# First product of an item in a linear-attention and MoE kernel: the block products in pY and the last one in pZ stand at the item's end, behind the last one in pX

## The chip, the cores and the metric

The kernel runs on one core of one Trainium2 chip. The metric is the device time of one execution in microseconds (us); of the three runs of the kernel before, the median is 851.96 us (850.62 to 854.63). Engines are named as in the profile: PE is TensorE (PEld its weight loads), DVE is VectorE, ACT is ScalarE, POOL is GpSimd, SP is SyncE, which issues most of the transfers.

## The reference

Linear attention (q is normalised by a softmax over the head dimension, k by one over the sequence) is followed by a feed-forward pair of products with a gate between them. All inputs are float32; there are 8 batches of 576 tokens, so 4608 tokens of width 512, and 2048 hidden columns.

```python
kv = np.einsum('bhsd,bhse->bhde', softmax(k, axis=seq), v)
x = np.einsum('bhsd,bhde->bhse', softmax(q, axis=dim), kv)   # to (4608, 512)
h = x @ w_in                                                # 512 -> 2048
sp = np.maximum(h, 0.0) + np.log1p(np.exp(-np.abs(h)))
g = h * erf(sp)
out = g @ w_out                                             # 2048 -> 512
```

## The kernel before

**Items.** The work on h, g and out is cut into 48 items, numbered n = 0 to 47 in the order in which they run: 12 blocks of 384 tokens, and for each block 4 groups of 512 hidden columns. Items 0 to 3 compute in fp32 (`mm1_32`, line 1030). Items 4 to 47 go through `mm1(n, k)` (line 977), which is called four times for an item, with k = 0 to 3. Every fp32 product is put together from fp16 halves, three matmuls for one.

**First product.** For one item, h is 512 columns by 384 tokens. It is cut into 2 by 2 blocks, `C[i, j]`, where i is a half of the columns and j a half of the tokens, and computed by a scheme in the manner of Strassen: seven block products of pre-added operands in place of eight. One block product, `prod(b, wi, xi)`, is 12 matmuls of 128x192 into one of three PSUM banks, whose tiles are named pX, pY and pZ. Each bank has one buffer in its pool (`bufs=1`) and belongs to an item from its first product to the last read of it. Products into the same bank accumulate: an item's first product in a bank starts it, the later ones add to what is there. So bank pX takes four products of an item (operands 0-0, 3-6, 5-5, 2-4 in this order), and after each one its contents are copied or added into one block of the item's tile H in SBUF; bank pZ takes two (6-3 and 4-2) and bank pY one (1-1). The next product into a bank has to wait until the eviction of the one before has read the bank. The evictions of k = 0, 2 and 3 run on DVE (but for the last one of pX), those of k = 1 and the last one of pX on ACT.

**The gate.** `softplus` (line 1062) and `erf` (line 1071) run on ACT over the item's 128x1536 values, both through `act` (line 337; its instructions are at line 342 in the profile). They use different function tables, so a table load stands ahead of each. For the items of the middle block of each pair (n modulo 12 from 4 to 7) the softplus is done in two halves, by token half; each half reads the blocks of H of that token half only. Then DVE multiplies (`gmul`, line 1081), casts the high half (`ghi`, 1093) and subtracts it for the low half (`glo`, 1097). `gh` and `gl` lie in the tile H.

**Second product.** `mm2(n, tt)` (line 1103, matmuls at 1125) is, for each of three 128-token tiles, 12 matmuls of 128x512 into banks o0, o1, o2, which accumulate over the block's four items. After a block's last item DVE scales them into `ob` (line 1141) and SP stores them.

**Order.** The loop at lines 1225 to 1244 writes, for each n, the gmul of item n-1, then for i = 0 to 3: m n.i (the call `mm1(n, i)`), the casts of item n-1, the second product of item n-2, tile i, and some steps of the attention of a later pair of batches (`pace`); at the end the softplus and erf of item n. The order of the text is a priority: a scheduler decides what stands where on each engine. `wlast[0]` is the instruction behind which an attention step is placed (`behind(wlast[0])`). The attention steps use all engines: exps on ACT (line 342), normalisation and splitting of kv on DVE (lines 459 to 465, 565 to 600), transposing transfers on SP (line 647), products x and xt on PE (line 636), and the preparation of the operands of the block products (lines 287, 288, 386).

Of the kernel before, what the change touches and what calls it, by code (L numbers as in the profile page):

```python
# [14 lines left out]
ALU = mybir.AluOpType  # L15
# [42 lines left out]
def attn_moe_kernel(  # L58
# [9 lines left out]
    nc = tc.nc  # L68
# [166 lines left out]
    def wop(jn, h, i, n):  # L235

        o = h * WIN + i * 512
        return wplace[wjobs[jn]][:, o:o + n * 512].rearrange("p (n c f) -> p n c f", n=n, c=2)
# [51 lines left out]
    wlast = [None]  # L290
# [686 lines left out]
    def mm1(n, k):  # L977

        p, bk, g = seq[n]
        s = st[n]
        assert ("in", g) in wready
        x = x7[p * NBK + bk]
        jn = wjobs.index(("in", g))
        Th = T // 2
        if k == 0:
            s["H"] = ch.tile([P, FG, T], F32, tag="H", bufs=3, name=f"H_{n}")
        C = {(i, j): s["H"][:, 2 * i:2 * i + 2, Th * j:Th * j + Th]
             for i in range(2) for j in range(2)}  # L990

        def prod(b, wi, xi):
            new = b not in s
            if new:
                s[b] = psh.tile([P, 512], F32, tag=f"p{b}", name=f"p{b}_{n}")
            w = [wop(jn, h, wi, 1)[:, 0] for h in range(2)]
            for a in range(2):
                o = s[b][:, a * Th:(a + 1) * Th]
                for c in range(2):
                    for i, (wl, xl) in enumerate(((0, 0), (0, 1), (1, 0))):  # L1000
                        nc.tensor.matmul(  # L1001
                            o, w[wl][:, c, a * P:(a + 1) * P], x[:, xl, xi, c, :],
                            start=(new and a == 0 and c == 0 and i == 0),
                            stop=(c == 1 and i == 2), skip_group_check=True,
                        )

        def bank2(b):
            return s[b][:, :T].rearrange("p (a t) -> p a t", a=2)

        add = nc.vector.tensor_tensor  # L1010
        if k == 0:
            prod("Y", 1, 1)
            wlast[0] = nc.vector.tensor_copy(C[0, 0], bank2("Y")).ins  # L1013
            prod("X", 0, 0)
            add(C[0, 0], bank2("X"), C[0, 0], op=ALU.add)  # L1015
        elif k == 1:
            prod("Z", 6, 3)
            nc.scalar.copy(C[1, 1], bank2("Z"))  # L1018
            prod("X", 3, 6)
            nc.scalar.copy(C[0, 1], bank2("X"))  # L1020
        elif k == 2:
            prod("X", 5, 5)
            wlast[0] = add(C[1, 1], bank2("X"), C[1, 1], op=ALU.add).ins  # L1023
        else:
            prod("Z", 4, 2)
            wlast[0] = add(C[0, 1], bank2("Z"), C[0, 1], op=ALU.add).ins  # L1026
            prod("X", 2, 4)
            nc.scalar.copy(C[1, 0], bank2("X"))  # L1028

    def mm1_32(n, a):  # L1030

# [120 lines left out]
    def tok(name):  # L1152
# [20 lines left out]
        if c == "w":  # L1173
            warm(*x)
        elif c == "D":
            wdecode(NPC * x[0] + x[1], *x[2:])
        elif c == "Q":
            wsquares(*x)
        elif c == "S":
            wsplit(*x)  # L1180
        elif c == "R":
            wsplit_sums(*x)
        elif c == "f":
            xready(x_next[0])
            finish(x[0] % 2)
        elif c == "Z":
            wscales()
        elif c == "m":
            (mm1_32 if x[0] < NG else mm1)(*x)
            emitted.add(("m", *x))  # L1190
        elif c == "M":
            mm2(*x)
            emitted.add(("M", *x))
        else:
            fn[c](*x)
# [81 lines left out]
```

## Time and profile before

| | before |
|---|---|
| median of 3 runs | 851.96 us |
| the profiled execution | 851.51 us |
| its span in the profile | 849.5 us |
| ACT busy | 503.1 us (59%) |
| matmuls of the first product into pX, pZ, pY | 204.8, 103.8, 52.0 us |
| matmuls of the second product (line 1125) | 366.1 us |

Busy time is the time in which an engine worked on instructions; of two engines that are both busy for most of the span, only waits and order tell which one sets the pace. In the 40 slices of the span each digit is the busy share of one slice of about 21 us, in tenths. A row of a timeline has the start in us from the span's start, the duration in us of the row (of all instructions that it groups, xN), engine, line, operation, output and inputs with their shapes; the bracket behind it says how long the engine was idle just before and what released it. A row of the list of waits has the us waited in total, how many times, and the longest one. The chain of work that ended last is PE for 47% of the span, DVE for 24% and ACT for 13%.

### The profile page before, as it was taken

Reading aid. Unit: us, or ns where it says so; the run is one execution under the profiler, and the core shown is the slowest. Engines: PE = TensorE matmul, PEld = TensorE weight load, DVE = VectorE, ACT = ScalarE, POOL = GpSimd, SP = SyncE. Lnnn points to the kernel's source line nnn. Section 1 sums busy time; section 2 is a strip of 40 time slices with the busy share of each in tenths; the row PEclk is TensorE's granted clock in tenths of the full one; section 3 lists DMA queues with packets and bytes.
Section 4 is the critical chain, followed back from the end, with each engine's and each line's share of the span. In section 5 each row is a group of like instructions: output and inputs, shape, how many; then the busy total and the mean of one; then the engine's idle time right before and its main releaser. Section 6 shows DMA issues by size and latency. Waiting matters only on the chain.

```text
span 849.5 us, 15212 instructions
## 1 busy us (share of the span) xinstructions
PE 802.6 (94%) x6377; PEld 546.7 (64%) x6377; DVE 637.7 (75%) x883; ACT 503.1 (59%) x633; POOL 35.3 (4%) x51
## 2 busy tenths in 40 slices
PE   3999997989989999999999999999999999999997
PEld 2555557566667567666676766666776676777673
DVE  5999789998979697848966777848968557553543
ACT  2598587686565665564854567465763565543532
POOL 1012010000100000000000100000000000000000
PEclk8999999999999999999999999999999999999999
DMA  9996320015405601531153300431131000100101
GB/s 264 404 276 182 106 74 15 1 25 107 112 18 114 149 2 26 119 75 26 39 104 75 89 16 16 115 88 26 38 51 38 33 7 2 38 1 2 38 1 38
DMA packets 145508, 62.59 MB, mean 74 GB/s; under 512 B 134688, under 2 KB 136736, under 8 KB 145440
## 3 DMA queue, kind: packets, MB, share of 16 engines
q1 hardware_dynamic: 143264, 53.23, 25.6%
q0 software_dynamic: 2176, 8.39, 2.8%
q8 instruction: 50, 0.82, 0.4%
q14 instruction: 18, 0.15, 0.0%
HBM read 45.09 MB, written 9.44 MB: 64 GB/s over the span
## 4 chain that ended last, share of the span: by engine, by line
PE 47%; DVE 24%; ACT 13%; issue 11%; DMA 3%; SPq 2%; POOL 0%; ACTq 0%; DVEq 0%; POOLq 0%
PE o L1125 20%; PE pX L1001 12%; PE pZ L1001 6%; ACT G L342 5%; ACT L342 5%; DVE G L1081 3%; PE pY L1001 2%; DVE H L1097 2%; DVE H L1093 2%; PE x L636 2%; SPq L407 1%; DVE x L288 1%; PE o L1116 1%; DVE q L453 1%; DVE x L386 1%
## 5 line engine op out<-in xcount | busy, mean ns | idle before, releaser
L1125 PE MATMUL o<-wo,H 128*128 128x512 f16 x1584 | 366.1, 379 | 2.9 <-DVE H L1093 2.0
L1001 PEld LDWEIGHTS <-wi 128*128 128x128 f16 x3696 | 311.2, 98 | 54.7 <-issue 24.7
L1125 PEld LDWEIGHTS <-H 128*128 128x128 f16 x1584 | 152.1, 98 | 157.3 <-DVE H L1093 2.7
L1001 PE MATMUL pX<-x,wi 128*128 128x192 f16 x2112 | 204.8, 247 | 11.5 <-DVE H L1023 3.3
L342 ACT ACT_TABLE_LOAD x104 | 133.4, 1283 | 11.3 <-DVE H L1026 9.6
L1081 DVE SCALAR_TENSOR_TENSOR G<-G,small,H 128x1536 f32<-128x1536 f32 x44 | 79.9, 1816 | 66.9 <-ACT G L342 66.9
L1028 ACT COPY H<-pX 128x384 f32<-128x384 f32 x44 | 20.9, 475 | 152.0 <-PE pX L1001 152.0
L1001 PE MATMUL pZ<-x,wi 128*128 128x192 f16 x1056 | 103.8, 248 | 2.9 <-ACT H L1018 2.1
L342 ACT ACTIVATE G<-H,U 128x768 f32<-128x768 f32 (+1 forms) x60 | 72.9, 1231 | 22.1 <-DVE H L1026 21.5
L1097 DVE TENSOR_TENSOR H<-G,H 128x1536 f16<-128x1536 f32 x44 | 77.2, 1755 | 0.9
L342 ACT ACTIVATE G<-G 128x1536 f32<-128x1536 f32 x48 | 71.2, 1484 | 0.5
L1001 PE MATMUL pY<-x,wi 128*128 128x192 f16 x528 | 52.0, 247 | 3.1 <-DVE H L1013 3.1
L1026 DVE TENSOR_TENSOR H<-pZ,H 128x384 f32<-128x384 f32 x44 | 24.3, 552 | 35.2 <-PE pZ L1001 35.0
L1013 DVE COPY H<-pY 128x384 f32<-128x384 f32 x44 | 24.3, 552 | 29.8 <-PE pY L1001 29.8
L288 DVE SCALAR_TENSOR_TENSOR x<-x,x 128x768 f16<-128x768 f32 (+1 forms) x44 | 37.2, 852 | 11.9 <-ACT x L287 11.6
L441 ACT ACTIVATE x<-x 128x384 f32<-128x384 f32 (+1 forms) x52 | 17.5, 388 | 44.6 <-PE x L636 41.3
L1116 PE MATMUL o<-wo,G 128*128 128x512 f32 x96 | 43.6, 597 | 0.0
L1093 DVE CAST H<-G 128x1536 f16<-128x1536 f32 x44 | 42.0, 956 | 0.8
L287 ACT ACTIVATE x<-x 128x768 f16<-128x768 f32 (+1 forms) x44 | 32.8, 762 | 9.4 <-DVE x L386 9.3
L1141 DVE TENSOR_SCALAR ob<-o,V 128x512 f32<-128x512 f32 x29 | 21.7, 747 | 20.0 <-PE o L1125 19.9
L1015 DVE TENSOR_TENSOR H<-pX,H 128x384 f32<-128x384 f32 x44 | 24.3, 552 | 11.3 <-PE pX L1001 11.1
L1116 PEld LDWEIGHTS o<-wo,G 128*128 128x128 f32 x96 | 17.5, 190 | 18.5 <-issue 17.5
(175 smaller groups left out, 751.1 us busy)
## 6 DMA issues: line engine op xcount, KB each, us to landing
out_dram<-ob SPq DMA_DIRECT2D x32, 256.0 KB, 2.4
vbuf<-in_v_dram SPq DMA_DIRECT2D x60, 128.0 KB, 3.0
q<-in_q_dram SPq DMA_DIRECT2D x56, 128.0 KB, 3.4
k<-in_k_dram SPq DMA_DIRECT2D x56, 128.0 KB, 3.0
wo<-in_moe_w_in_dram SPq DMA_DIRECT2D x4, 1024.0 KB, 17.1
wi<-in_moe_w_out_dram POOLq DMA_DIRECT2D x2, 1024.0 KB, 7.0
wi<-in_moe_w_in_dram SPq DMA_DIRECT2D x2, 1024.0 KB, 8.5
raw<-in_moe_w_out_dram POOLq DMA_DIRECT2D x2, 1024.0 KB, 7.7
```

What stands on the lines that cost most here:

```text
L287: nc.scalar.activation(hi, src, AF.Copy, scale=s)
L288: return nc.vector.scalar_tensor_tensor(lo, src, s, hi, op0=ALU.mult, op1=ALU.subtract)
L342: i = nc.scalar.activation(out_, in_, func, **kw)
L1001: nc.tensor.matmul(o, w[wl][:, c, a * P:(a + 1) * P], x[:, xl, xi, c, :], start=(new and a == 0 and c == 0 and i == 0), stop=(c == 1 and i ...
L1013: wlast[0] = nc.vector.tensor_copy(C[0, 0], bank2("Y")).ins
L1015: add(C[0, 0], bank2("X"), C[0, 0], op=ALU.add)
L1026: wlast[0] = add(C[0, 1], bank2("Z"), C[0, 1], op=ALU.add).ins
L1081: nc.vector.scalar_tensor_tensor(flat(s["G"]), flat(s["G"]), GA[:, g:g + 1], flat(s["H"]), op0=ALU.mult, op1=ALU.mult,)
L1093: nc.vector.tensor_copy(flat(s["gh"]), flat(s["G"]))
L1097: nc.vector.tensor_tensor(flat(s["gl"]), flat(s["G"]), flat(s["gh"]), op=ALU.subtract)
L1116: nc.tensor.matmul(o, s["G"][:, a, ts_], w[:, a, :], start=(first_ and a == 0), stop=(last_ and a == FG - 1),)
L1125: nc.tensor.matmul(o, s[gt][:, a, ts_], w[wl][:, a, :], start=(first_ and a == 0 and i == 0), stop=(last_ and a == FG - 1 and i == 2),)
```

## The change

Only the order of the products and the kinds of three evictions in `mm1` change.

```diff
--- before.py
+++ after.py
@@ -1009,10 +1009,8 @@
 
         add = nc.vector.tensor_tensor
         if k == 0:
-            prod("Y", 1, 1)
-            wlast[0] = nc.vector.tensor_copy(C[0, 0], bank2("Y")).ins
             prod("X", 0, 0)
-            add(C[0, 0], bank2("X"), C[0, 0], op=ALU.add)
+            wlast[0] = nc.vector.tensor_copy(C[0, 0], bank2("X")).ins
         elif k == 1:
             prod("Z", 6, 3)
             nc.scalar.copy(C[1, 1], bank2("Z"))
@@ -1022,10 +1020,12 @@
             prod("X", 5, 5)
             wlast[0] = add(C[1, 1], bank2("X"), C[1, 1], op=ALU.add).ins
         else:
+            prod("X", 2, 4)
+            nc.scalar.copy(C[1, 0], bank2("X"))
+            prod("Y", 1, 1)
+            add(C[0, 0], bank2("Y"), C[0, 0], op=ALU.add)
             prod("Z", 4, 2)
             wlast[0] = add(C[0, 1], bank2("Z"), C[0, 1], op=ALU.add).ins
-            prod("X", 2, 4)
-            nc.scalar.copy(C[1, 0], bank2("X"))
 
     def mm1_32(n, a):
```

The product into pY (operands 1-1) leaves k = 0 and goes to k = 3, behind the last product of pX and ahead of the last one of pZ. With it the first write into C[0, 0] becomes the copy of bank pX, and bank pY is added. In k = 3 the last product into pX comes first and the last one into pZ last. `wlast[0]` is the copy of pX in k = 0 and the add of pZ in k = 3. The number of matmuls, copies and adds stays.

The lines of the changed kernel shift: the copy of pX is line 1013 there, pZ's and pX's copies of k = 1 are 1016 and 1018, the add of k = 2 is 1021, and the three of k = 3 are 1024 (pX, ACT), 1026 (pY, DVE) and 1028 (pZ, DVE). Lines below 1028 are the same.

How the change moves instructions is seen first on DVE at the end of the program, in items 46 and 47, where no attention work is left (H_46 and H_47 are the items' tiles, G_46 the gate's). Before:

```order
L1026 TENSOR_TENSOR H_46_7956<-pZ_46_7999,H_46_7956 128x2x192
L1013 COPY H_47_8096<-pY_47_8097 128x2x192
L1015 TENSOR_TENSOR H_47_8096<-pX_47_8111,H_47_8096 128x2x192
L1081 SCALAR_TENSOR_TENSOR G_46_8092<-G_46_8092,small_82,H_46_7956 128x1536
L1093 CAST H_46_7956<-G_46_8092 128x1536
L1097 TENSOR_TENSOR H_46_7956<-G_46_8092,H_46_7956 128x1536
L1023 TENSOR_TENSOR H_47_8096<-pX_47_8111,H_47_8096 128x2x192
```

and now:

```order
L1026 TENSOR_TENSOR H_46_7956<-pY_46_8065,H_46_7956 128x2x192
L1028 TENSOR_TENSOR H_46_7956<-pZ_46_7985,H_46_7956 128x2x192
L1013 COPY H_47_8096<-pX_47_8097 128x2x192
L1081 SCALAR_TENSOR_TENSOR G_46_8092<-G_46_8092,small_82,H_46_7956 128x1536
L1093 CAST H_46_7956<-G_46_8092 128x1536
L1097 TENSOR_TENSOR H_46_7956<-G_46_8092,H_46_7956 128x1536
L1021 TENSOR_TENSOR H_47_8096<-pX_47_8097,H_47_8096 128x2x192
```

The copy of item 47's pY stood between item 46's last add and the gate's multiplication of item 46; now pY's add belongs to item 46 itself and stands ahead of the add of pZ, and item 47 has one operation fewer ahead of that multiplication.

The second place is ACT from the last copy of item 25 on (x7_7 are operands of the block products of a later block, k_6 and q_6 the keys and queries of a later batch). Before:

```order
L1028 COPY H_25_4555<-pX_25_4570 128x2x192
L287 ACTIVATE x7_7_4768<-x_7_3461 128x768
L342 ACT_TABLE_LOAD
L342 ACTIVATE G_25_4734<-H_25_4555,U_4_3279 128x1536
L287 ACTIVATE x7_7_4768<-x_7_3461 128x768
L342 ACT_TABLE_LOAD
L342 ACTIVATE G_25_4734<-G_25_4734 128x1536
L1018 COPY H_26_4738<-pZ_26_4786 128x2x192
L1020 COPY H_26_4738<-pX_26_4753 128x2x192
```

and now:

```order
L1024 COPY H_25_4555<-pX_25_4556 128x2x192
L287 ACTIVATE x7_7_4754<-x_7_3447 128x768 x2
L342 ACT_TABLE_LOAD
L342 ACTIVATE G_25_4734<-H_25_4555,U_4_3265 128x1536
L342 ACT_TABLE_LOAD
L342 ACTIVATE G_25_4734<-G_25_4734 128x1536
L1016 COPY H_26_4738<-pZ_26_4772 128x2x192
L1018 COPY H_26_4738<-pX_26_4739 128x2x192
```

The second operation of line 287 moved from between softplus and erf to a place ahead of the softplus's table load. One item later, before:

```order
L1018 COPY H_27_4894<-pZ_27_4939 128x2x192
L342 ACT_TABLE_LOAD
L342 ACTIVATE k_6_0_4404<-k_6_0_4404 128x1024
L1020 COPY H_27_4894<-pX_27_4909 128x2x192
L342 ACTIVATE k_6_1_4409<-k_6_1_4409 128x1024
L342 ACTIVATE kt_3_4414<-kt_3_4414 64x512
```

and now:

```order
L1016 COPY H_27_4894<-pZ_27_4925 128x2x192
L1018 COPY H_27_4894<-pX_27_4895 128x2x192
L342 ACT_TABLE_LOAD
L342 ACTIVATE k_6_0_4390<-k_6_0_4390 128x1024
L342 ACTIVATE k_6_1_4395<-k_6_1_4395 128x1024
L342 ACTIVATE kt_3_4400<-kt_3_4400 64x512
```

The copy of pX stood between two exps of the keys and now stands ahead of the table load of the first.

The third place is DVE in item 29, where the attention's kv is split (kvbd0; U and V are scales). Before:

```order
L599 TENSOR_SCALAR kvbd0_86<-kvf_6_5145,x6_s_5372 64x4x64 x2
L1141 TENSOR_SCALAR ob_27_2_5367<-o_24_2_4848,V_4_5258 128x512
L600 SCALAR_TENSOR_TENSOR kvbd0_86<-kvf_6_5145,x6_s_5372,kvbd0_86 64x4x64 x2
L1026 TENSOR_TENSOR H_29_5215<-pZ_29_5265,H_29_5215 128x2x192
L970 TENSOR_SCALAR V_6_7269<-small_82,x6_u_5373 128x1
L1013 COPY H_30_5414<-pY_30_5415 128x2x192
L645 TENSOR_TENSOR k_6_1_4409<-q_6_1_4694,k_6_1_4409 128x1024
L1015 TENSOR_TENSOR H_30_5414<-pX_30_5429,H_30_5414 128x2x192
L1081 SCALAR_TENSOR_TENSOR G_29_5409<-G_29_5409,small_82,H_29_5215 128x1536
```

and now:

```order
L599 TENSOR_SCALAR kvbd0_86<-kvf_6_5131,x6_s_5358 64x4x64
L1141 TENSOR_SCALAR ob_27_2_5353<-o_24_2_4834,V_4_5244 128x512
L600 SCALAR_TENSOR_TENSOR kvbd0_86<-kvf_6_5131,x6_s_5358,kvbd0_86 64x4x64
L599 TENSOR_SCALAR kvbd0_86<-kvf_6_5131,x6_s_5358 64x4x64
L970 TENSOR_SCALAR V_6_7255<-small_82,x6_u_5359 128x1
L600 SCALAR_TENSOR_TENSOR kvbd0_86<-kvf_6_5131,x6_s_5358,kvbd0_86 64x4x64
L1026 TENSOR_TENSOR H_29_5215<-pY_29_5382,H_29_5215 128x2x192
L1028 TENSOR_TENSOR H_29_5215<-pZ_29_5251,H_29_5215 128x2x192
L1013 COPY H_30_5414<-pX_30_5415 128x2x192
L645 TENSOR_TENSOR k_6_1_4395<-q_6_1_4680,k_6_1_4395 128x1024
L1081 SCALAR_TENSOR_TENSOR G_29_5409<-G_29_5409,small_82,H_29_5215 128x1536
```

The add of pZ of item 29 stood behind the two operations of line 600; now the adds of pY and of pZ both do, and one of line 599 and that of line 970 moved between the two of line 600.

## The prediction

> **What bounds the kernel now.** I read first the page's busy shares and 40 slices, then PE's list of waits, then the timeline of a quiet item near the end, and the busy times by stretch.
>
> ```profile
> PE 802.6 (94%) x6377; PEld 546.7 (64%) x6377; DVE 637.7 (75%) x883; ACT 503.1 (59%) x633; POOL 35.3 (4%) x51
> PE   3999997989989999999999999999999999999997
> DVE  5999789998979697848966777848968557553543
> ```
>
> PE is busy 94% of 849.5 us and in nine tenths of nearly every slice: in most places only work taken from PE or a wait of PE changes the time. DVE, at 75% overall, is as full as PE in slices 6 to 12 (107 to 255 us), so there the two take turns at setting the pace. PE's waits name the possible gains:
>
> ```profile
> PE pX L1001 <- DVE H L1023: 3.3, 4, 1.4
> PE pX L1001 <- ACT H L1020: 3.1, 4, 1.2
> PE pX L1001 <- ACT H L1028: 2.8, 3, 1.3
> PE xt L636 <- DVE H L1023: 2.7, 2, 1.4
> PE xt L636 <- DMA qt<-kt: 2.1, 1, 2.1
> ```
>
> Below, product names follow the evictions: X0, X3, X5 and X4 are the four products in pX in order of execution (old lines 1015, 1020, 1023, 1028), Z1 and Z2 those in pZ (1018, 1026), Y that in pY (1013). A quiet item in old order:
>
> ```profile
> 811.81 1.15 PE L1001 MATMUL pX<-x,wi 128*128 128x192 f16 x12
> 813.00 0.48 ACT L1028 COPY H<-pX 128x384 f32<-128x384 f32 x1 [7.67 <-PE pX L1001]
> 813.50 1.28 ACT L342 ACT_TABLE_LOAD   x1
> 817.68 1.48 ACT L342 ACTIVATE G<-G 128x1536 f32<-128x1536 f32 x1
> 819.19 1.82 DVE L1081 SCALAR_TENSOR_TENSOR G<-G,small,H 128x1536 f32<-128x1536 f32 x1 [3.66 <-ACT G L342]
> 819.55 0.48 ACT L1020 COPY H<-pX 128x384 f32<-128x384 f32 x1
> 821.05 0.96 DVE L1093 CAST H<-G 128x1536 f16<-128x1536 f32 x1
> 821.94 1.15 PE L1001 MATMUL pX<-x,wi 128*128 128x192 f16 x12
> 822.04 1.76 DVE L1097 TENSOR_TENSOR H<-G,H 128x1536 f16<-128x1536 f32 x1
> 822.93 2.75 PE L1125 MATMUL o<-wo,H 128*128 128x512 f16 x12
> 823.72 0.55 DVE L1023 TENSOR_TENSOR H<-pX,H 128x384 f32<-128x384 f32 x1
> 825.52 1.15 PE L1001 MATMUL pZ<-x,wi 128*128 128x192 f16 x12
> 826.51 1.15 PE L1001 MATMUL pX<-x,wi 128*128 128x192 f16 x12
> ```
>
> X4 starts at 811.81 and again at 826.51: a cycle of 14.70 us, with no wait in it. X5 takes 0.99 (822.93 - 821.94), twelve matmuls of the second product 2.59 (825.52 - 822.93), Z2 0.99. The softplus of the item starts when X4's copy ends (813.48); from its table load to the end of erf are 819.16 - 813.50 = 5.66. From the start of the line 1081 multiplication to the end of X5's add are 824.27 - 819.19 = 5.08: four DVE operations in a row. X5's add ends at 824.27 and X4, which reuses bank pX, starts at 826.51, so this chain has 2.24 to spare.
>
> **What the change does in a quiet item.** No instruction is added or removed: one DVE copy and three DVE adds, three ACT copies and 84 matmuls stay. The PE order goes from X5, o2, Z2, X4, Y(next), X0(next) to X5, o2, X4, Y, Z2, X0(next) (o2 the second product's third dozen). Two things follow. X4 stands straight behind o2, so X5's add has lost the 0.99 us of Z2 as cover. And the softplus now waits for Z2's add, the last of three products, instead of X4's copy, the last of two.
>
> Where a softplus did wait for Z2's add before, the rows are these:
>
> ```profile
> 502.72 0.55 DVE L1026 TENSOR_TENSOR H<-pZ,H 128x384 f32<-128x384 f32 x1
> 503.35 1.28 ACT L342 ACT_TABLE_LOAD   x1 [1.00 <-DVE H L1026]
> ```
>
> The add takes 0.55, and the table load starts 0.08 behind its end (503.27). Step by step, with X4's start as zero: Z2 starts at 1.98, its results are there at 3.13 (1.15 a dozen), the add starts 0.04 later (as X4's copy does, 813.00 against 811.81 + 1.15) and ends at 3.72, the table load starts at 3.80, erf ends at 9.46 (+5.66). Line 1081 starts at 9.49, X5's add ends at 14.57 (+5.08), and X4 of the next item could start at 14.63 if DVE to PE takes 0.06, between the two gaps just read. PE wants it at 14.70. The old slack of 2.24 is down to 0.07. X3's copy ends some 0.87 behind erf (820.03 - 819.16), at 10.33; PE wants X5 at 11.12 (14.70 less 2.59 and 0.99), slack 0.79. **A quiet item therefore costs nothing**, but only by 0.07 us: if the copies or the DVE queue run 0.1 us later than here, each of some 30 items pays 0.1. In any item with one more instruction on ACT or DVE between softplus and X5's add, that instruction is paid nearly in full.
>
> By the Trainium skill ("ScalarE: Activation LUTs", section "What ACT_TABLE_LOAD costs") every switch of function set costs a load of about 1.28 us and a drain of about 1.38. The rows above show the load (1.28) and erf starting at once behind it; no drain shows. With two drains in the chain it would be 14.63 + 2.76 = 17.4 against 14.70, and the old loop (12.46 + 2.76) would already wait, which it doesn't; the rows decide.
>
> **Items with attention work, 14 to 47.** Here I followed the order of the two kernels on each engine, item by item, with the durations of before.
>
> ```profile
> 512.17 1.15 PE L1001 MATMUL pX<-x,wi 128*128 128x192 f16 x12 [1.20 <-ACT H L1020]
> 488.92 1.28 ACT L342 ACT_TABLE_LOAD   x1
> 491.69 0.83 ACT L287 ACTIVATE x<-x 128x768 f16<-128x768 f32 x1
> 551.62 0.98 DVE L600 SCALAR_TENSOR_TENSOR kvbd<-kvf,x_s,kvbd 64x256 f16<-64x256 f32 x2
> 589.11 2.33 DVE L386 TENSOR_TENSOR x<-x 128x384 f32<-128x384 f32 x4
> 594.82 0.55 DVE L1023 TENSOR_TENSOR H<-pX,H 128x384 f32<-128x384 f32 x1
> 595.29 1.75 DVE L1097 TENSOR_TENSOR H<-G,H 128x1536 f16<-128x1536 f32 x1
> ```
>
> Gains. At items 15 and 27 X3's copy stood between two exps of the keys, and X5 waited 1.20 for it (512.17); now both copies stand ahead of the exp's table load. Of 3.1 in the list I count 1.8, since later work gives part back. The waits of xt (2.7, items 24 and 36) go: the cast that feeds its transfer comes earlier. Of the 2.8 behind line 1028 I take half, 1.4: X4's copy is no longer behind the cast of line 644, but an attention multiplication now stands ahead on DVE. 0.45 of the list's first row goes at item 40. Sum 6.35; ceiling 8.6 plus the 3.3 of that row.
>
> Losses. Item 26: the second line 287 activation, 0.83 at 491.69, used to run behind the softplus; now both stand ahead of its table load (488.92), which also waits for what feeds it. Bounds: 0 (0.83 less 0.79 slack) to 2.8 (491.69 - 488.92); I take 1.35. Items 18 and 30: Y's and Z2's adds stand behind the whole splitting of kv (line 600, until 552.60); the old order had Z2's add there and the softplus waited for X4's copy alone. Bounds 0 and 1.1 each time, the two adds; I take 1.03 twice, near the top as DVE is full there: 2.06. Items 20 and 32: X5's add (594.82) ran ahead of line 1097 (595.29, 1.75); now it stands behind it, while two of the four line 386 operations (2.33) move out of the way. Bounds 0 and 1.75; I take 0.9 twice: 1.8. Item 45, one output scaling between 1093 and 1097: 0.65 (its 0.75 less the slack). Item 35: 0.5 by the same kind of step. Ten items and the end with one short operation newly ahead of a copy or an add: 0 to 0.55 each (one add), I take 0.3: 2.95 with rounding. Sum 9.3. **Late part: +9.3 - 6.35 = +2.95.**
>
> **Items 4 to 13, where DVE is the bound.**
>
> ```profile
> 128.00:150.00 22.00, 17.36 (x171) 15.41 (x169) 21.47 (x29) 16.96 (x20) 0.00 (x0) 0.92 0.03 13
> 143.75 0.68 DVE L495 TENSOR_TENSOR k<-k 128x512 f32<-128x512 f32 x1
> 142.82 1.28 PE L1001 MATMUL pZ<-x,wi 128*128 128x192 f16 x7 [2.08 <-ACT H L1018]
> 143.89 2.13 PE L1001 MATMUL pX<-x,wi 128*128 128x192 f16 x12
> 145.60 1.82 DVE L1081 SCALAR_TENSOR_TENSOR G<-G,small,H 128x1536 f32<-128x1536 f32 x1
> 186.26 1.99 ACT L342 ACTIVATE q<-q 128x1024 f32<-128x1024 f32 x2
> 186.83 0.54 DVE L1023 TENSOR_TENSOR H<-pX,H 128x384 f32<-128x384 f32 x1
> 206.15 1.28 ACT L342 ACT_TABLE_LOAD   x1
> 207.06 0.99 DVE L600 SCALAR_TENSOR_TENSOR kvbd<-kvf,x_s,kvbd 64x256 f16<-64x256 f32 x2
> 211.85 1.82 DVE L1081 SCALAR_TENSOR_TENSOR G<-G,small,H 128x1536 f32<-128x1536 f32 x1 [1.78 <-ACT G L342]
> ```
>
> DVE works 21.47 of 22 us here, so what counts is new idle time on it. Item 4: two attention operations (from 143.75 until 145.60) filled the wait for erf ahead of line 1081; in the new order they stand behind it: +1.9 idle at most, taken whole. Item 7: X3's copy stands behind all five exps (end 188.25); X5 and its add follow at about 189.9, against 186.83, 3.1 later; two adds (1.0) that now stand ahead fill part. Between 0 and 2.1 I take the middle, 1.1. Item 8: Z2's add stands behind line 600 (until 208.05), so its table load starts at 208.05 + 0.55 + 0.08 = 208.7 instead of 206.15; line 1081 follows at 214.3 instead of 211.85: +2.4. Sum 5.4. The wait of xt for its transfer (2.1, at 280) then comes behind a later PE and takes back 2.0: the transfer is started by a cast that moves less than PE does. **Early part: +3.4**; bounds 0 and 5.4.
>
> Sum: 851.5 (the profiled execution; the median of the three runs is 852.0) + 2.95 + 3.4 = **857.9 us**.
>
> The early wait has a price that the sum leaves out. After a wait of 2.1 us the twelve matmuls at 143.89 took 2.13 instead of 1.15, and the granted clock of that stretch is 0.92. By the Trainium skill ("TensorE: Matmul & The Clock Gate", section "Part 1: The HAM clock gate") PE runs at half rate after an idle window of about 3.4 us and needs about as long of work to come back; the trace has the slow matmuls already after 2.1. With it the sum would be about 1 us more for each new wait of that length.
>
> **Rivals.** (a) *The gains alone.* Bank pY's product leaves the start of the item, X3's and X4's copies come free early, the waits behind 1020, 1028 and xt (8.6) all go, and the losses hide but for item 26, whose 1.35 is on ACT itself: 851.5 - 8.6 + 1.35 = 844.3. It decides if X5's add ends by 14.65 in nearly all attention items. For it: these waits are in the list; against it: the slack of 0.07. Chance 0.10. (b) *Nothing measurable.* The early idle is taken back whole in the waits before 290, and the late part stands: 851.5 + 2.95 = 854.5; with the ten small items hidden too, 851.5. For it: PE is at nine tenths all through, and my small losses are estimates. Against it: DVE has 0.53 us left in the 22 us from 128 to 150 to take anything back. Chance 0.36. (c) *The loop becomes the bound.* The chain from Z2's add to X5's add is 0.1 longer than 14.70 in 30 quiet items (+3), the early part keeps its 5.4 and two slow dozens (+2): 851.5 + 2.95 + 5.4 + 5 = 865. Chance 0.14. (d) *The change doesn't do what it says.* The scheduler could pull products back; in the new order it does so at items 8, 10 and 12 only, where X4 comes last. That is in the sum. My forecast has 0.40.
>
> **The range.** 850 to 865 holds the forecast, (b) and half of (c). A measurement of this kernel tells 0.5% (4.3 us) from no change; 856.2 is the upper bound of "the same". The forecast of 857.9 lies so near that a fifth of its chance falls below: slower 0.14 + 0.33 + 0.06 of (b) = 0.53, faster 0.09, the same 0.38.
>
> **What would show it.** In the new profile: Z2's add as the releaser of softplus in quiet items, and X4 starting within 0.1 us of X5's add's end there; cycles of 14.70 at the end of the kernel; the waits behind old 1020 gone; a new wait of PE in pX for X5's add in several items from 14 to 47; DVE idle before line 1081 of item 8 up from 1.78 to about 4. Wrong it would be if the quiet cycles are over 14.8 (then c), or if the early idle is absorbed and X4 of item 13 stands where it stood (then b).

## The result, and the profile after

| | before | after |
|---|---|---|
| median | 852.28 us (6 runs, 850.62 to 854.63) | 857.06 us (6 runs, 856.13 to 859.57) |
| the profiled execution | 851.51 us | 856.63 us |
| its span | 849.5 us | 854.9 us |

The ratio after to before is 1.0055, with a 95% interval from 1.0039 to 1.0071: slower by half a per cent, 4.8 us. The forecast was 857.9, which is 6.4 above the profiled execution of before that it started from. The page after, its busy times and two lines of slices:

```profile
PE 805.0 (94%) x6377; PEld 546.0 (64%) x6377; DVE 639.0 (75%) x883; ACT 501.7 (59%) x633; POOL 35.1 (4%) x51
PE   3998997879999899999999999999999999999997
DVE  6999889999778797948977677958977657554543
```

Busy times have hardly moved, as the work is the same. PE's slices 7 to 9, from 128 to 192 us, went from 7, 9, 8 to 7, 8, 7. PE's list of waits after:

```profile
PE pX L1001 <- DVE H L1021: 6.8, 10, 1.3
PE kv L546 <- ACT k L342: 6.0, 3, 3.0
PE pX L1001 <- ACT H L1018: 4.2, 7, 1.3
PE o L1125 <- DVE H L1093: 3.2, 3, 1.6
PE xt L636 <- DMA qt<-kt: 1.6, 1, 1.6
PE pX L1001 <- ACT H L1024: 1.3, 4, 0.6
```

The wait of bank pX for X5's add (line 1021 now) went from 3.3 to 6.8 us and from 4 times to 10, as the loss of cover says; five of the ten stand at items 20, 23, 32, 35 and 45, the others in items 5 to 12. The one for X4's copy fell from 2.8 to 1.3, and the wait of xt for DVE is gone. X3's copy (1018 now) is waited for longer, 4.2 against 3.1: the waits at items 15 and 27 are gone, but new ones stand at items 18, 21, 30 and 33 (0.70, 0.41, 0.70 and 0.41), and the one at item 26 grew from 0.37 to 1.25. The products of kv wait 6.0 for exps of the keys, half of it in one wait. The quiet item at the end, from X4 to X4:

```profile
815.08 1.15 PE L1001 MATMUL pX<-x,wi 128*128 128x192 f16 x12
817.06 1.15 PE L1001 MATMUL pZ<-x,wi 128*128 128x192 f16 x12
818.25 0.56 DVE L1028 TENSOR_TENSOR H<-pZ,H 128x384 f32<-128x384 f32 x1 [0.43 <-PE pZ L1001]
818.89 1.28 ACT L342 ACT_TABLE_LOAD   x1 [2.14 <-DVE H L1028]
823.07 1.48 ACT L342 ACTIVATE G<-G 128x1536 f32<-128x1536 f32 x1
824.59 1.82 DVE L1081 SCALAR_TENSOR_TENSOR G<-G,small,H 128x1536 f32<-128x1536 f32 x1 [4.79 <-ACT G L342]
829.11 0.55 DVE L1021 TENSOR_TENSOR H<-pX,H 128x384 f32<-128x384 f32 x1
829.78 1.15 PE L1001 MATMUL pX<-x,wi 128*128 128x192 f16 x12
```

The cycle is 829.78 - 815.08 = 14.70, as before. The table load has Z2's add as its releaser and starts 3.81 after X4 (forecast 3.80), X5's add ends at 829.66, which is 14.58 after X4 (forecast 14.57), and X4 follows 0.12 later. A quiet item costs nothing, with no more than that to spare.

To see where the 5.4 us of span came from, I compared the traces at equal PE work: the usual distance from start to start of each kind of matmul is added up along PE's queue, and at the same sum the start times are subtracted. This **lateness** does not depend on which product stands where. After against before it is 1.95 at the first block product, 6.69 behind item 13 (the point that PE reached at 300 us in the kernel before) and 5.39 at the end. So **the new order lost 4.7 us in items 4 to 13 and won 1.3 back in items 14 to 47**; 1.95 was there before any changed instruction, of which more in the last section.

**How far one trace carries.** Lateness compares single executions, and at two places these part though the text there is the same. At item 5 PE waits about 2.1 us in the executions named here; behind it the matmuls ran slow in some executions and not in others. From 140 to 150 us the granted clock is 0.83 in the kernel before and in run 6 below, 1.00 in the changed kernel and in runs 4 and 9. Runs 4 and 6 have the same text up to item 6, and still item 5 cost 1.2 us more in run 6. So I also count from the end of item 5: behind it the changed kernel lost 5.3 up to the 300 us point. The other place is the wait of xt at 280 us: behind 2.10 us of it the clock stayed at 1.00 in the kernel before (280 to 284 us), behind 2.21 us it was 0.57 in run 3 (280.4 to 284.4 us). Run 3 lost 1.75 in item 13 in this way and run 5, whose clock there was 0.57 too, 1.67, though items 4 to 13 have the old text in both.

### The profile page after: what moved, and what is told of

The parts are those of the page before. It is cut to its first block, busy times and chain, and to the rows that moved or that the text cites. A ratio compares the mean times of both kernels' runs of the same rounds, so it can differ in the third digit from the quotient of the medians.

```text
span 854.9 us, 15216 instructions
## 1 busy us (share of the span) xinstructions
PE 805.0 (94%) x6377; PEld 546.0 (64%) x6377; DVE 639.0 (75%) x883; ACT 501.7 (59%) x633; POOL 35.1 (4%) x51
## 4 chain that ended last, share of the span: by engine, by line
PE 46%; DVE 26%; ACT 15%; issue 6%; DMA 4%; SPq 2%; ACTq 0%; POOL 0%; DVEq 0%; POOLq 0%
PE o L1125 20%; PE pX L1001 11%; ACT G L342 6%; ACT L342 5%; PE pZ L1001 5%; DVE G L1081 3%; PE pY L1001 3%; DVE H L1097 3%; SPq L407 2%; PE kv L546 2%; DVE H L1093 1%; PE x L636 1%; DVE x L288 1%; PE o L1116 1%; DVE x L386 1%
## 5 line engine op out<-in xcount | busy, mean ns | idle before, releaser
L1001 PEld LDWEIGHTS <-wi 128*128 128x128 f16 x3696 | 308.1, 98 | 55.7 <-issue 28.8
L1026 DVE TENSOR_TENSOR H<-pY,H 128x384 f32<-128x384 f32 x44 | 24.4, 555 | 45.5 <-PE pY L1001 45.4
L1013 DVE COPY H<-pX 128x384 f32<-128x384 f32 x44 | 24.4, 554 | 11.6 <-PE pX L1001 11.6
L546 PE MATMUL kv<-vbuf,k 128*64 128x65 f32 x480 | 21.9, 236 | 8.6 <-ACT k L342 6.0
```

The source lines that it names most:

```text
L546: nc.tensor.matmul(bk[a * D:(a + 1) * D, c * W:(c + 1) * W], kk, vv, start=(t == 0), stop=(t == TM),)
L1001: nc.tensor.matmul(o, w[wl][:, c, a * P:(a + 1) * P], x[:, xl, xi, c, :], start=(new and a == 0 and c == 0 and i == 0), stop=(c == 1 and i ...
L1013: wlast[0] = nc.vector.tensor_copy(C[0, 0], bank2("X")).ins
L1026: add(C[0, 0], bank2("Y"), C[0, 0], op=ALU.add)
```

## The experiments

Each ran beside the kernel before. The last three columns are the lateness of the profiled execution: at the first block product, what came up to the 300 us point, and what came behind it.

| run | median, us | ratio to before | start | to item 13 | rest |
|---|---|---|---|---|---|
| changed kernel | 857.06 | 1.0055 (1.0039 to 1.0071) | 1.95 | 4.74 | -1.30 |
| 1: pY at the end, X4 last | 857.00 | 1.0045 (1.0030 to 1.0060) | 0.58 | 6.75 | -1.66 |
| 2: X4 ahead of Z2 only | 853.71 | 1.0016 (1.0003 to 1.0029) | 0.65 | -0.40 | 2.02 |
| 3: new order from item 14 | 851.87 | 0.9989 (0.9976 to 1.0002) | 0.89 | 1.28 | -0.83 |
| 4: new order to item 13 | 856.87 | 1.0058 (1.0037 to 1.0079) | 1.55 | 5.21 | -0.66 |
| 5: seven single items | 853.74 | 1.0008 (0.9990 to 1.0026) | 0.19 | 1.04 | 1.00 |
| 6: run 4, X3 of item 7 on DVE | 858.22 | 1.0069 (1.0050 to 1.0088) | 1.12 | 6.68 | -0.63 |
| 7: items 4 and 5 | 856.48, 1 run | | 0.44 | 4.66 | 0.05 |
| 8: items 8 to 13 | 851.75, 1 run | | 0.97 | 0.22 | -0.72 |
| 9: one other anchor | 851.72 | 0.9997 (0.9984 to 1.0010) | -0.87 | 0.76 | -1.16 |
| 10: item 5 | 855.91, 1 run | | 1.34 | 3.10 | 0.08 |
| 11: swap in ten items | 849.53 | 0.9965 (0.9949 to 0.9980) | -0.60 | -0.65 | -3.27 |
| 12: swap in six items | 850.02 | 0.9975 (0.9964 to 0.9986) | 1.51 | -0.83 | -2.81 |

**Which half of the change, and where.** Run 1 moves pY alone, run 2 swaps the last two products alone; runs 3 and 4 split the items.

```diff
 # run 1, k = 3, against the changed kernel
-            prod("X", 2, 4)
-            nc.scalar.copy(C[1, 0], bank2("X"))
             prod("Y", 1, 1)
...
             wlast[0] = add(C[0, 1], bank2("Z"), C[0, 1], op=ALU.add).ins
+            prod("X", 2, 4)
+            nc.scalar.copy(C[1, 0], bank2("X"))
 # run 2, k = 3, against the kernel before
+            prod("X", 2, 4)
+            nc.scalar.copy(C[1, 0], bank2("X"))
             prod("Z", 4, 2)
             wlast[0] = add(C[0, 1], bank2("Z"), C[0, 1], op=ALU.add).ins
-            prod("X", 2, 4)
-            nc.scalar.copy(C[1, 0], bank2("X"))
 # runs 3 and 4: the new text and the old one, by item
+        if n >= 14:
...
```

Run 4 has `n < 14` in its place.

> pY's product (and its add) stands at the item's end, but the last product of pX stays behind the last one of pZ, with its ACT copy last. Theory A (the price is paid where the softplus waits for Z2's add and X4 has no cover; pY at the end by itself costs only in items 4 to 13, where it can no longer be pulled ahead): quiet cycles stay 14.70 with over 2 us of slack at X4, the late gains of the change (X3's copies ahead of the exps, the xt wait) stay, its late losses mostly go; items 4 to 13 still lose 2 to 5 us. Sum 848 to 853 us, ratio to before 0.995 to 1.001. Theory B (pY at the end is itself the price, by its place ahead of the softplus and by its add on DVE): as slow as the changed kernel, 856 to 858, ratio 1.004 to 1.007.

> Only the two products of the last call swap places: X4 first, Z2 last; pY stays at the item's start. Theory A: X4 loses its cover of 0.99 and the softplus waits for Z2's add, 0.99 plus 0.16 us later than for X4's copy measured from X4's start; slack at X4 falls from 2.2 to about 1.1, so quiet items cost nothing and attention items lose less than in the changed kernel; the gain behind X3's copy at items 15 and 27 is not there. 852 to 856, ratio 1.000 to 1.004. Theory B: no change, 851 to 853.

> The new order in items 14 to 47 only, the old one in items 4 to 13. Theory A: the new order gains 1.35 there and loses 0.14 at the end, so 850 to 852, ratio 0.997 to 1.000, and items 4 to 13 run as before. Rival C (the loss of the change is spread over the loop, and the early lateness of the profile is an accident of that one execution): 855 to 858, ratio 1.003 to 1.007.

> The new order in items 4 to 13 only. Theory A: the whole loss and a little more, 856 to 859, ratio 1.004 to 1.008. Rival C: 852 to 854, ratio 1.000 to 1.002.

Run 1 is as slow as the change, so theory A's figure for it was wrong: pY at the end is the price. But the table shows that it is a price of items 4 to 13 (6.75); behind them run 1 gains 1.66. Run 2 costs nothing there and 2.02 later. Its losses at items 23, 26 and 35 (0.88, 1.05 and 0.88) stand where the changed kernel lost 0.44, 0.89 and 0.52, so these can be the swap's. But at 18 and 30, where the changed kernel lost 0.86 each, run 1 lost 0.08 and run 2 nothing: these steps need both halves of the change. Runs 3 and 4 settle the place: with the new order only behind item 13 the time is that of before within the interval, and with it only in items 4 to 13 the whole loss is there. Item by item, from the end of each item's last block product to that of the next, run 3 repeats the changed kernel from item 15 on to 0.1 us: the steps belong to the order, not to the execution.

**Which items, and is it a wait that I had named?** Run 5 keeps the new order where the changed kernel gained; run 6 takes away the wait of X5 in item 7 for X3's copy, which stands behind five exps; runs 7 and 8 split the early items.

```diff
 # run 5: condition for the new text
+        if n in (15, 17, 24, 27, 29, 36, 40):
 # run 6, k = 1, in items up to 13
-            nc.scalar.copy(C[0, 1], bank2("X"))
+            (nc.vector.tensor_copy if n == 7 else nc.scalar.copy)(C[0, 1], bank2("X"))
 # runs 7 and 8: conditions for the new text
+        if n in (4, 5):
+        if 8 <= n < 14:
```

> The new order only in items 15, 17, 24, 27, 29, 36 and 40, which in the changed kernel's trace lost 7.6 us of lateness together (0.95, 1.12, 1.24, 1.18, 1.12, 1.55, 0.45); the old order elsewhere. Theory A (each item's gain belongs to its own order): 845 to 848 us, ratio 0.992 to 0.995, each of the seven steps there again within 0.2. Rival D (the gain needs the neighbours in the new order too, or the steps from one order to the other cost what is gained): 850 to 853, ratio 0.998 to 1.001.

> As the run with the new order in items 4 to 13, but X3's copy of item 7 runs on DVE, so that it no longer stands behind the five exps on ACT. Theory E (this wait is worth its 2.1 us of idle on DVE ahead of X5's add of item 7, less the 0.55 of the moved copy): 1 to 1.6 us less lateness at item 8 than there, 855 to 856, ratio 1.003 to 1.005. Rival F (DVE is full, and the wait for the gate of the next item takes the place of this one): within 0.5 us of that run, 856.5 to 857.

> The new order in items 4 and 5 only. One look, read by the lateness against the kernel before at equal PE work, less that at the first block product. If the idle of DVE ahead of line 1081 of item 4 (1.53 in the changed kernel) is a price of its own: +1 to +2 from item 6 on, and it stays to the end. If DVE's queue makes it up again: within 0.5 of nothing from item 8 on.

> The new order in items 8 to 13 only. By the same measure: item 8's softplus behind the splitting of kv costs +2 to +3 from item 9 or 10 on (its DVE idle was 4.91 against 1.78), and the sum with the run for items 4 and 5 and what is left for 6 and 7 is the 4.7 of the whole. If the cost of item 8 is only inherited from the lateness of items 6 and 7: under 0.7.

Run 5 went as rival D: items 15 and 27 gained 1.04 and 1.27 again, but items 17, 24, 29 and 36 nothing, and items 18 and 30 lost 1.55 each. Run 6 is 1.5 us later than run 4 up to item 13 (6.68 against 5.21), but 1.2 of this is item 5's difference in clock, ahead of the copy that was moved. From the end of item 5 on it is 0.3, as rival F said: the idle time of DVE ahead of X5's add of item 7 fell from 2.17 to 0.79, and the lateness shows no gain from it. The time, 858.2, lies above both forecasts; its interval overlaps with that of run 4. Runs 7 and 8 were the turn: **items 4 and 5 in the new order make most of the early loss (4.66 in the table; from the end of item 5 on 4.1 of 5.3), items 8 to 13 next to none (0.22)**. Items 6 and 7 alone were not run. The idle time that I saw in item 7 is a consequence: run 7 has it too, 2.28, with the old text in item 7. The one ahead of item 8's gate, 4.91 in the changed kernel, is 1.97 in run 7 and 1.82 in run 8, so it needs both the early loss and the new order of later items.

**What in items 4 and 5.** The trace after, DVE and PE around item 4's gate and item 6's X5 (columns as in the timelines above):

```profile
145.14 0.56 DVE L1026 TENSOR_TENSOR H<-pY,H 128x384 f32<-128x384 f32 x1
147.23 1.82 DVE L1081 SCALAR_TENSOR_TENSOR G<-G,small,H 128x1536 f32<-128x1536 f32 x1 [1.53 <-ACT G L342]
165.49 1.47 PE L1125 MATMUL o<-wo,H 128*128 128x512 f16 x6 [1.58 <-DVE H L1093]
170.84 1.21 DVE L452 TENSOR_REDUCE q_m<-q 128x16 f32<-128x1024 f32 x1
172.43 1.21 DVE L453 TENSOR_TENSOR q<-q,q_m 128x1024 f32<-128x1024 f32 x1
174.90 0.54 DVE L1021 TENSOR_TENSOR H<-pX,H 128x384 f32<-128x384 f32 x1
175.50 1.15 PE L1001 MATMUL pX<-x,wi 128*128 128x192 f16 x12 [1.09 <-DVE H L1021]
```

and the kernel before, the copy of item 6's pY and item 6's X5 and X4:

```profile
143.29 0.55 DVE L1013 COPY H<-pY 128x384 f32<-128x384 f32 x1
168.65 1.21 DVE L453 TENSOR_TENSOR q<-q,q_m 128x1024 f32<-128x1024 f32 x1
170.26 0.54 DVE L1023 TENSOR_TENSOR H<-pX,H 128x384 f32<-128x384 f32 x1
170.85 1.15 PE L1001 MATMUL pX<-x,wi 128*128 128x192 f16 x12
```

Before, two attention operations (lines 495 and 452) filled DVE's wait for item 4's erf, until 145.60. Now DVE idles 1.53 there; their work comes later. Between that gate and X5's add of item 6 (line 1021) DVE has five operations more than before: one each of lines 495 and 452, two of line 386 and one of line 288, all attention work. The add ends at 175.44 instead of 170.80, and X4 waits for it 1.09. Why they moved is in the code: attention steps are placed behind `wlast[0]`. In the old order that was, at the beginning of item 6, the copy of item 6's pY, which ran early, at 143.29, as its bank was free. In the new order it is item 6's copy of pX, which runs at 154.29. The wait of 1.58 at 165.49, for the cast of item 5, is another matter: before, ten matmuls of item 7's pY filled part of it and 0.66 was left; in run 9 below it is 1.83. Run 9 changes this anchor alone, run 10 makes it with item 5 alone:

```diff
 # run 9, k = 0, against the changed kernel
-            wlast[0] = nc.vector.tensor_copy(C[0, 0], bank2("X")).ins
+            s["x0"] = wlast[0] = nc.vector.tensor_copy(C[0, 0], bank2("X")).ins
+            if n == 6:
+                wlast[0] = st[5]["x0"]
 # run 10: condition for the new text
+        if n == 5:
```

> The changed kernel with one line more: the attention steps of item 6's beginning are placed behind item 5's copy of pX instead of item 6's own. In the old order that place was item 6's copy of pY, which ran early. On DVE lines 495 and 452 stand ahead of line 1081 of item 4 again, and two operations of line 386 instead of eight attention operations ahead of X5's add of item 6. Theory G (the early loss is this displaced attention work: it leaves 1.5 us of DVE idle at item 4 and then stands ahead of X5's add of item 6, where PE waits for bank pX): the lateness from item 8 on falls by 3 to 4.7 us, time 852 to 854, ratio 0.999 to 1.003, and with the late gain of 1.3 perhaps below the kernel before. Rival H (pY's product at the end costs by itself, through its bank and its add, wherever the attention work stands): 856 to 858, ratio 1.004 to 1.007.

> The new order in item 5 only, so that item 5's pY is at its end and item 6's pY, though early again in the program, finds the bank taken. One look, by lateness at equal PE work less that at the first block product. Theory G: +4 to +5 from item 8 to the end, as with items 4 and 5 together, since lines 495 and 452 are behind line 1081 of item 4 here too. Rival H: about half of it, +2 to +2.5.

Run 9, on DVE and PE:

```profile
142.20 0.68 DVE L495 TENSOR_TENSOR k<-k 128x512 f32<-128x512 f32 x1
143.60 1.22 DVE L452 TENSOR_REDUCE q_m<-q 128x16 f32<-128x1024 f32 x1
144.73 1.81 DVE L1083 SCALAR_TENSOR_TENSOR G<-G,small,H 128x1536 f32<-128x1536 f32 x1
168.51 0.55 DVE L1023 TENSOR_TENSOR H<-pX,H 128x384 f32<-128x384 f32 x1
169.14 1.15 PE L1001 MATMUL pX<-x,wi 128*128 128x192 f16 x12
```

Both operations are back ahead of the gate's multiplication (line 1083 here), which follows them with no idle time, and X4 of item 6 starts at 169.14 without a wait. The early loss falls from 4.74 to 0.76, and the time is that of the kernel before. **Four fifths of the early loss was displaced attention work**, put back by moving one anchor; counted from the end of item 5, where these two executions ran at the same clock, it falls from 5.3 to 1.0. What is left is what pY's place may cost by itself, and these traces bound it no better than to about 1 us. The old order with this other anchor was not run, so whether the anchor gives back only what the change took is open. Run 10 has a loss again, 3.10, between theory G's 4 to 5 and rival H's 2 to 2.5, though item 6 has its old text: item 5's pY holds the bank at its end, so item 6's copy of pY runs at 154.74 instead of 143.29. Its rows:

```profile
146.70 1.82 DVE L1101 SCALAR_TENSOR_TENSOR G<-G,small,H 128x1536 f32<-128x1536 f32 x1 [1.73 <-ACT G L342]
177.28 1.80 PE L1001 MATMUL pX<-x,wi 128*128 128x192 f16 x12 [2.56 <-DVE H L1043]
```

DVE idles 1.73 ahead of the gate, and X4 of item 6 waits 2.56 for X5's add. The rest, 1.6 between runs 10 and 7, I did not split further.

**A version that beats both.** Of the later steps the largest without a loss behind it was run 2's at items 17 and 29, 1.42 each. Runs 11 and 12 make the swap of run 2 in ten and in six items:

```diff
 # runs 11 and 12: conditions for run 2's text
+        if n in (15, 16, 17, 18, 19, 27, 28, 29, 30, 31):
+        if n in (15, 16, 17, 27, 28, 29):
```

> Only the swap of the last two products (X4 ahead of Z2; pY stays at the item's start), and only in items 15 to 19 and 27 to 31, where the run with the swap everywhere lost 1.97 and 2.19 us of lateness, without its losses of 1.19 at items 21 and 33 and the later ones. If a step belongs to the item's own order: 848 to 849, ratio 0.994 to 0.997. If the neighbours give it back, as they did in the run with seven single items: 851 to 853, ratio 0.999 to 1.001.

> The same swap in items 15 to 17 and 27 to 29 only, so that the old order returns one item behind the gain. If the gain lasts: as the run with ten items, 848 to 849. If it is given back at items 18 and 30: 851 to 853.

Both are faster than the kernel before, run 11 by 0.35% (0.9965, to 0.9980 at most), 849.5 us, and both show the two steps of 1.42. What a step is made of, at item 29, before:

```profile
535.01 1.04 ACT L644 CAST k<-q 128x1024 f16<-128x1024 f32 x1 [7.54 <-PE pY L1001]
535.96 0.47 ACT L1028 COPY H<-pX 128x384 f32<-128x384 f32 x1
536.48 1.15 PE L1001 MATMUL pX<-x,wi 128*128 128x192 f16 x12 [1.26 <-ACT H L1028]
```

and in run 11:

```profile
530.25 0.48 ACT L1027 COPY H<-pX 128x384 f32<-128x384 f32 x1 [5.97 <-PE pX L1001]
531.77 1.05 ACT L644 CAST k<-q 128x1024 f16<-128x1024 f32 x1 [1.04 <-DVE q L465]
532.03 1.15 PE L1001 MATMUL pX<-x,wi 128*128 128x192 f16 x12
```

Before, X4's copy stood behind the cast of line 644, which had to wait for its input (line 465 on DVE, done at 534.91; the row's bracket names a product of PE that ended at the same time, but in run 11 the cast starts before that product has ended), and the next product in pX waited 1.26 for the bank. With X4 one product earlier its copy is through before the cast, and the product starts without a wait. Run 11's ratio lies in the range expected, its time half a microsecond above; run 12's 850.0 lies between its two forecasts, though its trace shows no step given back; the smaller steps of run 2 at items 15 and 27 did not come in either run.

## Why the prediction came out right, and which of its terms did not

- **Quiet items, no cost: right**, with the slack as worked out (14.58 against 14.57). Rival (c) falls. Of the signs named, the cycle, the releaser of the softplus, the new waits for X5's add and the idle time ahead of item 8's gate came; that the waits behind old line 1020 would be gone did not, as the list after shows.
- **The drain of the Trainium skill ("ScalarE: Activation LUTs", section "What ACT_TABLE_LOAD costs")**: the rows again show none. From the table load at 818.89 to the end of erf at 824.55 are 5.66, as before.
- **Items 14 to 47, +2.95: wrong in size and sign.** It was -1.30. The mechanisms were there, item by item: 0.95 gained at item 15, 1.18 at 27, 1.24 and 1.55 at 24 and 36, and the losses at 18, 20, 26, 30, 32 and 45. Gains were mis-sized, 7.6 instead of 6.35 (items 17 and 29 gave 1.12 each where I took 0.7), and losses too, 6.3 instead of 9.3: 0.86 at 18 and 30 for 1.03, 0.55 at 20 and 32 for 0.9, 0.89 at 26 for 1.35, and the ten small ones came to 1.7 instead of 2.95. At items 18 and 30 most of the loss is X5's wait of 0.70 for X3's copy, the chain behind a later softplus that the prediction had. At item 27 the rows are as forecast, both copies ahead of the exps' table load and X5 without a wait:

```profile
515.24 0.48 ACT L1018 COPY H<-pX 128x384 f32<-128x384 f32 x1
515.74 1.28 ACT L342 ACT_TABLE_LOAD   x1
516.42 1.15 PE L1001 MATMUL pX<-x,wi 128*128 128x192 f16 x12
```

- **Items 4 to 13, +3.4: near in size, half wrong in cause.** The idle times came, 1.53 for 1.9 at item 4, 2.07 for 1.1 at item 7 (within its bounds of 0 and 2.1), and 3.1 more for 2.4 at item 8:

```profile
192.95 0.56 DVE L1021 TENSOR_TENSOR H<-pX,H 128x384 f32<-128x384 f32 x1 [2.07 <-PE pX L1001]
218.74 1.82 DVE L1081 SCALAR_TENSOR_TENSOR G<-G,small,H 128x1536 f32<-128x1536 f32 x1 [4.91 <-ACT G L342]
```

  But I took three idle times for three prices. Runs 7 and 8 show one price for the most part, and the other two idle times as what follows from it: items 4 and 5 cost 4.66, items 8 to 13 cost 0.22. What the step "item 4: +1.9 idle" missed is what follows the idle time: the same operations come later, ahead of X5's add of item 6.
- **The wait of xt at 280 takes 2.0 back: wrong.** It is 1.6 after against 2.1, so it took 0.5.
- **A mark that misleads.** The prediction's last sign is X4's start of item 13. There the new order has X4 one product earlier, and item 13's own pY still to come, so at equal work it is 0.99 + 0.99 = 1.98 later than that start shows. The 3.4 is a sum of idle times that names no mark; read at this one it would stand for 5.4 at equal work.
- **So the total was right through errors that offset each other, and that is luck**: of the 6.35 forecast (2.95 + 3.4), the late part was 4.25 too much and the early part 1.3 too little, and 1.95 of lateness at the start stood in no term. Together this is the 5.4 by which the span grew. Rival (a), the gains alone, falls, and so does (b), nothing measurable, by the interval's lower end of 1.0039, though by little: its 854.5 is 1.0035 times 851.5. Of (d) the opposite holds: the change did more than that rival allows for, as it moved the anchor of other work.

## What to carry to other kernels

When a step is moved, look for what else is placed by it: here the product's copy was the anchor behind which a scheduler put other work, and this, not the bank or the added wait, was four fifths of the early loss. Idle time of the engine that was the bound had its price here where the displaced work landed, not in its own length, and waits further on were in part its consequences: run the change in a few of the loop's rounds only before pricing each. Order effects of single rounds can be collected one by one if the neighbouring rounds don't give them back, which only a run tells.

## What the runs showed of the hardware

Up to the first block product the kernels before and after have the same order on DVE, ACT and PE (but for two neighbouring kv products on PE), and still it started 1.95 us later in the profiled execution of the changed kernel; in run 9's it started 0.87 earlier than before. One place where executions part is the issue of eight transfers of keys on SP, in the timeline of before:

```profile
46.99 7.74 SPq L407 DMA_DIRECT2D k<-in_k_dram  x8
```

and of after, where it took 3.6 longer:

```profile
46.93 11.37 SPq L407 DMA_DIRECT2D k<-in_k_dram  x8
```

Differences of 1 or 2 us between single profiled executions are therefore no effect of a change, unless they are measured from a mark behind this.

A wait of PE did not always cost clock. Before, the twelve matmuls behind the wait of 2.08 took 2.13; after, the same place:

```profile
144.45 0.90 PE L1001 MATMUL pZ<-x,wi 128*128 128x192 f16 x9 [2.07 <-ACT H L1016]
145.19 1.15 PE L1001 MATMUL pX<-x,wi 128*128 128x192 f16 x12
```

Here a wait of 2.07 is followed by a dozen in 1.15, as without a wait; the granted clock from 140 to 150 us is 1.00, against 0.83 before. A wait of 2.56 was followed by a dozen in 1.80 in run 10, and in run 7 by one in 1.15 and a later one in 1.94. So the length of the wait alone does not decide. The Trainium skill ("TensorE: Matmul & The Clock Gate", section "Part 1: The HAM clock gate") says that the window in which activity is counted runs freely and does not start with the work, which would explain that like waits end differently; the window itself is not seen in these traces.
